# A channel gate on one pass over HBM: an early gate from one tile, loads on two queues, wide sums and a shorter last tile

## The chip, the cores and the metric

One core of a Trainium2 chip runs the kernel. The metric is device time in microseconds (us). "Span" is the time from the first to the last instruction in one profiled execution; the device time is about 1.8 us longer. All medians below are of runs on the chip, each kernel alternating with the kernel before on the same chip. A single-core program has no second die to compare with, so a run is called slow only by its time.

## The reference

```python
H = W = C = 384                      # x: (1, H, W, C) in bf16; w1d: one bf16 number
g = jnp.einsum("bhwc->bc", x) / (H * W)      # mean of each channel
s = jax.nn.sigmoid(g * w1d[0])               # k = 1: one weight
return x * s[:, None, None, :]
```

x holds 113.25 MB, and so does the output. The gate s depends on the mean of all of x, so an honest reading needs x twice: once for the mean, once for the product. Both kernels avoid the second reading. They take the mean of the first rows, compute an early gate `s_early`, multiply and store with it while the sums of the other rows go on, and at the end compare `s_early` with the true gate bit by bit in bf16. Only if they differ does a second pass run. By an estimate from the reference's inputs (x and w1d are normal numbers of spread 0.05) the gate lies so near 0.5 that one tile and all rows round to the same bf16 number.

## The kernel before

The 147,456 rows of 384 channels are cut into 1152 groups of 128 rows, one row for each partition ("rows" below are such groups; one is 768 bytes in each partition). A small planner records every operation with the memory it reads and writes and puts in the waits. The parts that matter:

```python
TILE = 45
AHEAD_TILES = 3
# ... cut ...
    sizes = split(n_rows, TILE)                   # 8 tiles of 45 rows, 18 of 44
    early_rows = sum(sizes[:AHEAD_TILES])
# ... cut ...
    def load(place, n, r0):
        plan.dma("sync", at(place, n), dram(x_rows, r0, n), writes=rows(place, n))

    def add_rows(place, n, bank, first, last):    # column sums: ones^T times each row
        for i in range(n):
            plan.op("tensor", lambda e, i=i: e.matmul(acc[bank][:, :C], ones[:], at(place + i, 1),
                    start=first and i == 0, stop=last and i == n - 1), ...)

    def put(place, n, r0):                        # gate in place, then store
        plan.op("vector", gate(place, n, s_early), ...)
        plan.final.append(
            plan.dma("scalar", dram(o_rows, r0, n), at(place, n), reads=rows(place, n)))

    ring = Ring(n_arena)                          # the room holds six tiles
    for k, n in enumerate(sizes):
        place = ring.take(n)
        while inside and any(p < place + n and place < p + m for p, m, _ in inside):
            put(*inside.pop(0))                   # gate and store the tile whose place is needed
        load(place, n, r0)
        add_rows(place, n, 0 if k < AHEAD_TILES else 1, ...)
        if k == AHEAD_TILES - 1:
            # ... copy the sums, s_early = sigmoid(sums * w / count) ...
    for tile in inside:
        put(*tile)
    # ... true sums, s_true, compare, set the flag of the second pass ...
```

Loads are issued from the sync engine's queue (q1 in the profile) and stores from the scalar engine's (q10).

## Time and profile before

| | before |
|---|---|
| device time, median of the first 3 runs | 532.59 us (532.49 to 532.88) |
| span of the profiled run | 530.9 us |
| bytes moved by DMA | 226.67 MB |
| matmuls | 1153 |
| first store issued | 55.0 us |
| last load landed | 482.8 us |

The page of the kernel before, the rows on the DMA and the engines. PE is the matmul engine, PEld its weight loads, DVE the vector engine, ACT the scalar engine and POOL the gpsimd engine, each with its busy time in us, share of the span and number of instructions; a row of a queue (q8, q14) gives packets, MB and the share of the 16 engines' time. The rows named DMA and GB/s are cut into 40 equal slices of the span: the first is the mean busy share of the 16 DMA engines in tenths, the second what they moved.

```profile
span 530.9 us, 2501 instructions
PE 241.9 (46%) x1153; PEld 127.3 (24%) x1153; DVE 236.8 (45%) x34; ACT 2.7 (1%) x4; POOL 0.3 (0%) x5
DMA  9999999999999999999999999999999999999996
GB/s 372 419 436 437 413 419 440 432 424 442 422 442 422 443 426 438 438 420 444 425 433 446 415 442 440 418 440 437 423 443 428 430 444 415 443 443 414 443 435 290
DMA packets 7502, 226.67 MB, mean 427 GB/s; under 512 B 834, under 2 KB 834, under 8 KB 834
q8 instruction: 9, 0.15, 0.1%
q14 instruction: 3, 0.02, 0.0%
```

Neither compute engine is half busy, and the DMA engines are never free. Read the DMA row before any chain of waits: the chain in this profile attributes 63% of the span to "another core or an unknown queue", which here is the time in which a store or load stood in its queue.

The windows view of the kernel before, with its line of headings; the last two numbers of a row are the DMA share and GB/s. A packet counts whole in the window in which it starts, so a share can come out a little over 1.

```profile
core 0: us, PE busy (x) PEld busy (x) DVE busy (x) ACT busy (x) POOL busy (x), PEclk, DMA share, GB/s
0.00:5.00 5.00, 0.16 (x1) 0.10 (x1) 0.39 (x3) 1.49 (x2) 0.30 (x5) 1.00 0.68 221
5.00:30.00 25.00, 15.68 (x82) 8.63 (x83) 0.00 (x0) 0.00 (x0) 0.00 (x0) 1.00 1.02 441
30.00:55.00 25.00, 18.27 (x100) 9.98 (x98) 9.77 (x3) 0.61 (x1) 0.00 (x0) 0.93 0.99 426
55.00:75.00 20.00, 9.89 (x48) 5.27 (x49) 20.00 (x3) 0.00 (x0) 0.00 (x0) 0.79 1.00 417
75.00:500.00 425.00, 197.92 (x926) 103.36 (x924) 203.73 (x23) 0.00 (x0) 0.00 (x0) 0.72 1.00 433
500.00:525.00 25.00, 0.00 (x0) 0.00 (x0) 2.87 (x5) 0.61 (x1) 0.00 (x0) 0.50 1.01 434
525.00:531.00 6.00, 0.00 (x0) 0.00 (x0) 0.00 (x0) 0.00 (x0) 0.00 (x0) 0.50 0.29 124
```

The share is 1 from 5 us to 525 us, whether loads run alone (to 55 us), loads with stores, or stores alone (after 483 us). The rate of 433 GB/s is a ceiling, not an average with holes in it. Only the first 5 us and the last 6 us are loose.

The DMA issues of the kernel before: queue, number, size, and median time from issue to landing.

```profile
arena<-in_x_dram SPq DMA_DIRECT2D x18, 4224.0 KB, 27.6
out_dram<-arena ACTq DMA_DIRECT2D x18, 4224.0 KB, 73.6
```

A load needs 27.6 us and a store 73.6, though each is 10 us of work for the 16 engines (4.325 MB / 433 GB/s). The rest is queueing; the stores are the ones that pile up.

The trace also keeps every single DMA packet with its start, duration, size and queue. A data packet here is one partition's share of a tile, 33,792 or 34,560 bytes, and takes 1251 or 1279 ns. The last packet that each of the 16 engines runs is the 4-byte semaphore write of the last store. Its end, sorted over the engines (us from the span's start; worked out from those records):

```
before  526.0 526.1 526.2 526.2 526.3 526.4 527.1 527.4 527.6 527.6 527.6 527.6 527.8 528.1 528.9 529.9
```

So the first engine is done 3.9 us before the last, and the span ends 0.9 us after the last one.

### The profile page before, as it was taken

The page shows a single profiled execution, that of the slowest core. Times are in us where ns is not written, and L with a number is a line of the kernel's source. Part 1 is how long each engine was busy: PE and PEld are TensorE (multiplying, and loading weights), DVE is VectorE, ACT ScalarE, POOL GpSimd, SP SyncE. Part 2 cuts the span into 40 slices and gives each one's busy share as a digit, 9 for nine tenths or more (in the row PEclk, how much of TensorE's full clock was granted, in tenths as well). Part 3 has the DMA queues.
Part 4 walks back from the last instruction along what each step waited for, and adds up shares of the span by engine and source line. Part 5 has one row for each costly group of instructions (what it writes and reads, how often), then busy time and mean ns, then how long its engine had stood idle before and what let it go on. Part 6 is the DMA issues. An engine that isn't in the chain of part 4 may idle for free.

```text
span 530.9 us, 2501 instructions
## 1 busy us (share of the span) xinstructions
PE 241.9 (46%) x1153; PEld 127.3 (24%) x1153; DVE 236.8 (45%) x34; ACT 2.7 (1%) x4; POOL 0.3 (0%) x5
## 2 busy tenths in 40 slices
PE   0979643326257256156156266256155265265000
PEld 0435312213123133023033133123033033133000
DVE  0005999561542642642642633642642633633800
ACT  1000000000000000000000000000000000000000
POOL 0000000000000000000000000000000000000000
PEclk9989867588576677686786775686786786676755
DMA  9999999999999999999999999999999999999996
GB/s 372 419 436 437 413 419 440 432 424 442 422 442 422 443 426 438 438 420 444 425 433 446 415 442 440 418 440 437 423 443 428 430 444 415 443 443 414 443 435 290
DMA packets 7502, 226.67 MB, mean 427 GB/s; under 512 B 834, under 2 KB 834, under 8 KB 834
## 3 DMA queue, kind: packets, MB, share of 16 engines
q1 hardware_dynamic: 3744, 113.25, 49.7%
q10 hardware_dynamic: 3746, 113.25, 49.5%
q8 instruction: 9, 0.15, 0.1%
q14 instruction: 3, 0.02, 0.0%
HBM read 113.25 MB, written 113.25 MB: 427 GB/s over the span
## 4 chain that ended last, share of the span: by engine, by line
another core or an unknown queue 63%; DMA 19%; DVE 7%; PE 3%; SPq 1%; issue 1%; ACT 0%; DVEq 0%
DMA arena<-in_x_dram 12%; DMA out_dram<-arena 8%; DVE arena L165 7%; PE acc L206 3%; SPq L91 1%; ACT s_true L273 0%; ACT s_early L255 0%; DVE total L281 0%; DVE total L249 0%; DVE wrong L289 0%; DVE total L267 0%; SPq L99 0%; DVE redo L295 0%; DVEq L99 0%
## 5 line engine op out<-in xcount | busy, mean ns | idle before, releaser
L206 PE MATMUL acc<-arena,ones 128*128 128x384 bf16 x1152 | 241.8, 381 | 248.1 <-DMA arena<-in_x_dram 248.1
L165 DVE TENSOR_TENSOR arena<-arena,s_early 128x16896 bf16<-128x16896 bf16 (+1 forms) x26 | 234.1, 9019 | 222.0 <-PE acc L206 221.3
L206 PEld LDWEIGHTS acc<-arena,ones 128*128 128x128 bf16 x1152 | 127.2, 112 | 362.3 <-DMA arena<-in_x_dram 257.8
L249 DVE COPY total<-acc 128x384 f32<-128x384 f32 x1 | 0.6, 557 | 42.1 <-PE acc L206 42.1
L273 ACT ACTIVATE s_true<-total,w_scaled 128x384 bf16<-128x384 f32 x1 | 0.6, 614 | 455.9 <-DVE total L267 455.9
L177 ACT ACT_TABLE_LOAD x1 | 1.3, 1283 | 1.3 <-PEq L373 1.3
L183 PE MATMUL acc<-w_one,ones 1*128 1x1 bf16 x1 | 0.2, 158 | 2.1 <-DMA w_one<-in_w1d_dram 2.1
L281 DVE TENSOR_TENSOR total<-s_true,s_early 128x384 f32<-128x384 uint16 x1 | 0.6, 559 | 0.7 <-ACT s_true L273 0.7
L255 ACT ACTIVATE s_early<-total,w_scaled 128x384 bf16<-128x384 f32 x1 | 0.6, 614 | 42.4 <-DVE total L249 42.4
L192 DVE TENSOR_SCALAR w_scaled<-acc 128x1 f32<-128x1 f32 x2 | 0.2, 154 | 1.3 <-PE acc L183 1.3
L183 PEld LDWEIGHTS acc<-w_one,ones 1*128 1x128 bf16 x1 | 0.1, 97 | 2.0 <-issue 2.0
L289 DVE TENSOR_REDUCE wrong<-total 128x1 f32<-128x384 f32 x1 | 0.6, 553 | 0.0
L267 DVE TENSOR_TENSOR total<-total,acc 128x384 f32<-128x384 f32 x1 | 0.5, 547 | 0.0
L173 DVE MEMSET ones<- 128x128 bf16 x1 | 0.2, 165 | 0.8 <-PEq L373 0.8
L177 ACT ACTIVATE warm<-warm 128x1 f32<-128x1 f32 x1 | 0.2, 202 | 0.0
L295 DVE CAST redo<-wrong 128x1 int32<-128x1 f32 x1 | 0.2, 154 | 0.0
L373 POOL MEMSET const-bfloat16-1.0<- 128x1 bf16 x1 | 0.1, 103 | 0.0
L373 POOL MEMSET const-uint8-127<- 128x1 uint8 x1 | 0.1, 103 | 0.0
L373 POOL MEMSET const-float32-1.0<- 128x1 f32 x1 | 0.1, 100 | 0.0
L172 POOL MEMSET warm<- 128x1 f32 x1 | 0.1, 99 | 0.3 <-POOLq L373 0.3
L373 POOL MEMSET const-float32-0.0<- 128x1 f32 x1 | 0.1, 99 | 0.2 <-issue 0.2
## 6 DMA issues: line engine op xcount, KB each, us to landing
arena<-in_x_dram SPq DMA_DIRECT2D x18, 4224.0 KB, 27.6
out_dram<-arena ACTq DMA_DIRECT2D x18, 4224.0 KB, 73.6
arena<-in_x_dram SPq DMA_DIRECT2D x8, 4320.0 KB, 30.2
out_dram<-arena ACTq DMA_DIRECT2D x8, 4320.0 KB, 58.7
w_one<-in_w1d_dram ACTq DMA_DIRECT2D x1, 0.0 KB
```

The source lines that it names most:

```text
L91: ("op", lambda e: e.dma_start(out, in_), self.pool[i], 16)
L165: return lambda e: e.tensor_tensor(v, v, s_b, ALU.mult)
L177: lambda e: e.activation(warm[:, 1:2], warm[:, 0:1], ACT_F.Sigmoid),
L183: lambda e: e.matmul(acc[2][:, 0:1], ones[0:1, :], w_one[0:1, 0:1], start=True, stop=True),
L206: lambda e, i=i: e.matmul(acc[bank][:, :C], ones[:], at(place + i, 1), start=first and i == 0, stop=last and i == n - 1,),
L249: lambda e: e.tensor_copy(total[:], acc[0][:, :C]),
L255: lambda e: e.activation(s_early[:], total[:], ACT_F.Sigmoid, scale=w_scaled[:, 0:1]),
L267: lambda e: e.tensor_tensor(total[:], total[:], acc[1][:, :C], ALU.add),
L273: lambda e: e.activation(s_true[:], total[:], ACT_F.Sigmoid, scale=w_scaled[:, 1:2]),
L281: lambda e: e.tensor_tensor(total[:], s_true[:].bitcast(U16), s_early[:].bitcast(U16), ALU.not_equal),
L289: lambda e: e.reduce_max(wrong[:], total[:], axis=mybir.AxisListType.X),
L373: nc = _bacc.Bacc("TRN2", target_bir_lowering=False, num_devices=1)
```

## The change

Its intent is to start storing sooner and to take waits out of the start and the tail. It takes `s_early` from the first tile of 44 rows; loads the first three tiles by halves on both queues; names six slots of 44 rows in place of the ring; sums 512 columns by one matmul instead of 384; makes the last two tiles 28 and 24 rows; and writes the product of the last tile into a slot that is free, so that the gate does not wait for the matmuls that read the tile.

```diff
-TILE = 45
-AHEAD_TILES = 3
+WIDE = 512
+EDGE, SLOT, BOTH = 44, 44, 3
@@ loads @@
+    def load(place, n, r0, queues=("sync",)):
+        of = dram(x_rows, r0, n)
+        i = 0
+        for queue, m in zip(queues, split(n, -(-n // len(queues)))):
+            plan.dma(queue, at(place + i, m), of[:, i * C : (i + m) * C], ...)
+            i += m
@@ sums: three banks, 512 columns each @@
-        for i in range(n):
-                    acc[bank][:, :C], ones[:], at(place + i, 1),
+        for i in range(n_wide):                      # n_wide = n * C // WIDE
+            bank = acc[group][i % 3]
+                    bank[:, :], ones[:],
+                    arena[:, start + i * WIDE : start + (i + 1) * WIDE],
@@ order @@
+    for k in range(BOTH):
+        load(places[k], sizes[k], starts[k], ("sync", "scalar"))
+    add_rows(places[0], sizes[0], 0, True, True)
+    add_banks(0, copy=True)                          # six small vector operations
+    # ... s_early ...
+    for k in range(1, len(sizes)):
+        if k >= n_slots:
+            j = k - n_slots
+            put(places[j], sizes[j], starts[j], places[j])
+        if k >= BOTH:
+            load(places[k], sizes[k], starts[k])
+        add_rows(places[k], sizes[k], 1, k == 1, k == last)
+    for k in range(len(sizes) - n_slots, last):
+        put(places[k], sizes[k], starts[k], places[k])
+    put(places[last], sizes[last], starts[last], places[last + 1 - n_slots])
```

(Shortened: some argument lists are written as "...", and the operations that compute and compare the gates are left out.)

More of the change, by code (lines that the diff above doesn't have):

```diff
@@ L108, in split @@
     return [n // k + (i < n % k) for i in range(k)]
-class Ring:
-    def __init__(self, size):
-        self.size, self.at = size, 0
-    def take(self, n):
-        if self.at + n > self.size:
-            self.at = 0
-        self.at += n
-        return self.at - n
-TILE = 45
-AHEAD_TILES = 3
+WIDE = 512
+EDGE, SLOT, BOTH = 44, 44, 3
 def bass_standalone__channel_attn_eca__vision_kernel(
@@ L134, in bass_standalone__channel_attn_eca__vision_kernel @@
     B, H, W, C = x.shape
-    assert B == 1 and C == ROW and (B * H * W) % P == 0
+    assert B == 1 and C == ROW and (B * H * W) % (4 * P) == 0
     n_rows = B * H * W // P
@@ L152, in bass_standalone__channel_attn_eca__vision_kernel @@
     arena = nc.alloc_sbuf_tensor("arena", [P, n_arena * C], BF16)
-    acc = [nc.alloc_psum_tensor(f"acc{i}", [P, 512], F32) for i in range(3)]
+    acc = [
+        [nc.alloc_psum_tensor(f"acc{g}_{i}", [P, WIDE], F32) for i in range(3)]
+        for g in range(2)
+    ]
+    w_all = nc.alloc_psum_tensor("w_all", [P, WIDE], F32)
     def at(r0, n):
@@ L160, in rows, with gate @@
         return [("sb", r) for r in range(r0, r0 + n)]
-    def gate(place, n, s):
+    def gate(to, place, n, s):
         s_b = s[:].unsqueeze(1).broadcast_to([P, n, C])
-        v = at(place, n).rearrange("p (t c) -> p t c", t=n)
-        return lambda e: e.tensor_tensor(v, v, s_b, ALU.mult)
-    sizes = split(n_rows, TILE)
-    early_rows = sum(sizes[:AHEAD_TILES])
-    plan = Planner(nc, "a", 50)
+        v, to_v = (at(r, n).rearrange("p (t c) -> p t c", t=n) for r in (place, to))
+        return lambda e: e.tensor_tensor(to_v, v, s_b, ALU.mult)
@@ new lines, in bass_standalone__channel_attn_eca__vision_kernel @@
+    n_slots = n_arena // SLOT
+    full, rest = divmod(n_rows - EDGE, SLOT)
+    if rest < EDGE:
+        full, rest = full - 1, rest + SLOT
+    sizes = [EDGE] + [SLOT] * full + [4 * q for q in split(rest // 4, EDGE // 4)]
+    assert sum(sizes) == n_rows and max(sizes) <= SLOT
+    plan = Planner(nc, "a", 50)
+    def load(place, n, r0, queues=("sync",)):
+        of = dram(x_rows, r0, n)
+        i = 0
+        for queue, m in zip(queues, split(n, -(-n // len(queues)))):
+            plan.dma(
+                queue,
+                at(place + i, m),
+                of[:, i * C : (i + m) * C],
+                writes=rows(place + i, m),
+            )
+            i += m
@@ new lines, in add_rows @@
+    def add_rows(place, n, group, first, last):
+        n_wide = n * C // WIDE
+        start = place * C
+        for i in range(n_wide):
+            bank = acc[group][i % 3]
+            plan.op(
+                "tensor",
+                lambda e, i=i, bank=bank: e.matmul(
+                    bank[:, :],
+                    ones[:],
+                    arena[:, start + i * WIDE : start + (i + 1) * WIDE],
+                    start=first and i < 3,
+                    stop=last and i >= n_wide - 3,
+                ),
+                reads=["ones"] + (rows(place, n) if i in (0, n_wide - 1) else []),
+                writes=[f"acc{group}"],
+                signal=i == n_wide - 1,
+            )
@@ new lines, in add_banks @@
+    def add_banks(group, copy):
+        for m, lo, hi in ((0, 0, C), (0, C, WIDE), (1, 0, 256), (1, 256, WIDE),
+                          (2, 0, P), (2, P, WIDE)):
+            c = (128 * m + lo) % C
+            part = total[:, c : c + hi - lo]
+            of = acc[group][m][:, lo:hi]
+            if copy and (m, lo) == (0, 0):
+                emit = lambda e, part=part, of=of: e.tensor_copy(part, of)
+            else:
+                emit = lambda e, part=part, of=of: e.tensor_tensor(
+                    part, part, of, ALU.add
+                )
+            plan.op("vector", emit, reads=[f"acc{group}", "total"], writes=["total"])
@@ new lines, in put, with weight @@
+    def put(place, n, r0, to):
+        plan.op(
+            "vector",
+            gate(to, place, n, s_early),
+            reads=["s_early"] + rows(place, n),
+            writes=rows(to, n),
+        )
+        plan.final.append(
+            plan.dma("scalar", dram(o_rows, r0, n), at(to, n), reads=rows(to, n))
+        )
+    def weight():
+        plan.op(
+            "scalar",
+            lambda e: e.activation(warm[:, 1:2], warm[:, 0:1], ACT_F.Sigmoid),
+            reads=["warm"],
+            writes=["warm1"],
+        )
+        plan.op(
+            "tensor",
+            lambda e: e.matmul(
+                w_all[:, 0:1], ones[0:1, :], w_one[0:1, 0:1], start=True, stop=True
+            ),
+            reads=["ones", "w_one"],
+            writes=["w_all"],
+        )
+        for i, n in enumerate((sizes[0], n_rows)):
+            plan.op(
+                "vector",
+                lambda e, i=i, n=n: e.tensor_scalar_mul(
+                    w_scaled[:, i : i + 1], w_all[:, 0:1], 1.0 / float(P * n)
+                ),
+                reads=["w_all"],
+                writes=[f"w_scaled{i}"],
+            )
@@ L172, in bass_standalone__channel_attn_eca__vision_kernel @@
+    starts = [sum(sizes[:k]) for k in range(len(sizes))]
+    places = [k % n_slots * SLOT for k in range(len(sizes))]
+    last = len(sizes) - 1
     plan.op("gpsimd", lambda e: e.memset(warm[:, 0:1], 0.0), writes=["warm"])
     plan.op("vector", lambda e: e.memset(ones[:], 1.0), writes=["ones"])
-    plan.dma("scalar", w_one[0:1, 0:1], w1d.unsqueeze(0), writes=["w_one"])
+    for k in range(BOTH):
+        load(places[k], sizes[k], starts[k], ("sync", "scalar"))
+        if k == 0:
+            plan.dma("scalar", w_one[0:1, 0:1], w1d.unsqueeze(0), writes=["w_one"])
@@ L175, in bass_standalone__channel_attn_eca__vision_kernel @@
+    weight()
+    add_rows(places[0], sizes[0], 0, True, True)
+    add_banks(0, copy=True)
     plan.op(
         "scalar",
-        lambda e: e.activation(warm[:, 1:2], warm[:, 0:1], ACT_F.Sigmoid),
-        reads=["warm"],
-        writes=["warm1"],
-    )
-    plan.op(
-        "tensor",
-        lambda e: e.matmul(
-            acc[2][:, 0:1], ones[0:1, :], w_one[0:1, 0:1], start=True, stop=True
-        ),
-        reads=["ones", "w_one"],
-        writes=["acc2"],
-    )
-    for i, n in enumerate((early_rows, n_rows)):
-        plan.op(
-            "vector",
-            lambda e, i=i, n=n: e.tensor_scalar_mul(
-                w_scaled[:, i : i + 1], acc[2][:, 0:1], 1.0 / float(P * n)
-            ),
-            reads=["acc2"],
-            writes=[f"w_scaled{i}"],
-        )
@@ L199, in load @@
-    def load(place, n, r0):
-        plan.dma("sync", at(place, n), dram(x_rows, r0, n), writes=rows(place, n))
-    def add_rows(place, n, bank, first, last):
-        for i in range(n):
-            plan.op(
-                "tensor",
-                lambda e, i=i: e.matmul(
-                    acc[bank][:, :C],
-                    ones[:],
-                    at(place + i, 1),
-                    start=first and i == 0,
-                    stop=last and i == n - 1,
-                ),
-                reads=["ones"] + (rows(place, n) if i in (0, n - 1) else []),
-                writes=[f"acc{bank}"],
-                signal=i == n - 1,
-            )
@@ L218, in put @@
-    def put(place, n, r0):
-        plan.op(
-            "vector",
-            gate(place, n, s_early),
-            reads=["s_early"] + rows(place, n),
-            writes=rows(place, n),
-        )
-        plan.final.append(
-            plan.dma("scalar", dram(o_rows, r0, n), at(place, n), reads=rows(place, n))
-        )
-    ring = Ring(n_arena)
-    inside = []
-    r0 = 0
-    for k, n in enumerate(sizes):
-        place = ring.take(n)
-        while inside and any(
-            p < place + n and place < p + m for p, m, _ in inside
-        ):
-            put(*inside.pop(0))
-        load(place, n, r0)
-        inside.append((place, n, r0))
-        if k < AHEAD_TILES:
-            add_rows(place, n, 0, k == 0, k == AHEAD_TILES - 1)
-        else:
-            add_rows(place, n, 1, k == AHEAD_TILES, k == len(sizes) - 1)
-        r0 += n
-        if k == AHEAD_TILES - 1:
-            plan.op(
-                "vector",
-                lambda e: e.tensor_copy(total[:], acc[0][:, :C]),
-                reads=["acc0"],
-                writes=["total"],
-            )
-            plan.op(
-                "scalar",
-                lambda e: e.activation(
-                    s_early[:], total[:], ACT_F.Sigmoid, scale=w_scaled[:, 0:1]
-                ),
-                reads=["total", "w_scaled0", "warm1"],
-                writes=["s_early"],
-            )
@@ L261, in bass_standalone__channel_attn_eca__vision_kernel @@
-    for tile in inside:
-        put(*tile)
-    plan.op(
-        "vector",
-        lambda e: e.tensor_tensor(total[:], total[:], acc[1][:, :C], ALU.add),
-        reads=["total", "acc1"],
-        writes=["total"],
-    )
+        lambda e: e.activation(
+            s_early[:], total[:], ACT_F.Sigmoid, scale=w_scaled[:, 0:1]
+        ),
+        reads=["total", "w_scaled0", "warm1"],
+        writes=["s_early"],
+    )
+    for k in range(1, len(sizes)):
[5 more added lines that the diff above has]
+        add_rows(places[k], sizes[k], 1, k == 1, k == last)
@@ L271, in bass_standalone__channel_attn_eca__vision_kernel @@
+    for k in range(len(sizes) - n_slots, last):
+        put(places[k], sizes[k], starts[k], places[k])
+    put(places[last], sizes[last], starts[last], places[last + 1 - n_slots])
+    add_banks(1, copy=False)
     plan.op(
@@ L302, in bass_standalone__channel_attn_eca__vision_kernel @@
     again = Planner(nc, "b", 50)
-    ring = Ring(n_arena)
-    r0 = 0
-    for n in sizes:
-        place = ring.take(n)
+    for place, n, r0 in zip(places, sizes, starts):
         again.dma("sync", at(place, n), dram(x_rows, r0, n), writes=rows(place, n))
@@ L309, in bass_standalone__channel_attn_eca__vision_kernel @@
             "vector",
-            gate(place, n, s_true),
+            gate(place, place, n, s_true),
             reads=rows(place, n),
@@ L316, in bass_standalone__channel_attn_eca__vision_kernel @@
         )
-        r0 += n
     for token in again.final:
```

## The prediction

> **What bounds the kernel now.** The DMA engines, from first packet to last. The page counts 226.67 MB; the windows view shows DMA share 1.00 and about 433 GB/s in nearly every 5 us stretch from 60 to 525 us, with loads and stores mixed (55 to 483) and stores alone (483 to 526). Vector is 45% busy, matmul 46%; neither is on the path. The Trainium skill, "DMA: Bandwidth & Descriptors", section "Where 436 GB/s comes from", gives 435.2 GB/s as the ceiling of the 16 ports; the trace agrees within 1%. So 226.67 MB / 433 GB/s = 523.5 us of the 530.9 us span cannot be touched: both kernels move the same bytes once.
>
> **The rest is 7.4 us.** The DMA records show it: first packet at 1.7 us; first packets take 2.0 to 2.6 us instead of 1.28; when stores start (57 us) one load packet per engine takes about 1.9 us; each of nine 16 KB fetches of PE instructions takes about 0.93 us on one engine and makes the next packet 0.4 us longer; so the engines end between 526.0 and 529.9 us, and 0.9 us more passes until the last instruction.
>
> **What the change does.**
> - Early gate from one tile: the first store's issue moves from 55 us to about 34 (tile lands near 12, 33 wide matmuls about 9.5, six small vector sums about 2.5 estimated from 0.56 for 384 columns, activation 0.6, gate 9.0). But the DMA engines were already full with six queued loads; stores only take their share sooner. The stores-only tail shrinks from 47 us to about 35 (last load lands about 493). Worth 0.
> - Two queues for three tiles: same 16 engines (same page, "Issuing engines are not separate DMA queues": it saves only issue time). An issue costs 0.33 us here, hidden behind 10 us transfers. Worth 0 to 0.3 us.
> - Six slots: the old ring also held six tiles (six loads issued without a wait). Worth 0.
> - Wide sums: 864 matmuls in place of 1152, same columns, so PE stays near 240 us, off the path. Side effect: fewer instruction fetches (9 to about 7), which trims the engine that ends last by perhaps 1 us.
> - 40 more packets per engine (halved tiles, one more tile). From 33792 B in 1251 ns and 34560 B in 1279 I estimate 19 ns fixed each: costs 0.8 us.
> - Last tile 24 rows, gated into a free slot without waiting for its sums: saves about 13 us between last load and its store's issue (matmul 8.8, gate 9.0 to 5), but some 20 MB of stores wait then, so nothing starves in either kernel. Worth 0.
> Sum: -1 us, give or take 1.5.
>
> **Prediction:** 531.3 us, range 529.3 to 533.4. Faster by over 2% 0.01, same 0.96, slower by over 2% 0.03.
>
> **What would show it.** DMA share still 1.00 and 433 GB/s from 5 to 520 us; first store issued at 30 to 38 us; last load landing at 490 to 497; loads' median time to landing rising from 28 to about 55 us and stores' falling from 73 to about 50 (slots hold waiting loads in place of waiting stores); PE busy unchanged within 10%; six or seven 16 KB instruction packets; engines' ends spread over 2 to 4 us.
>
> **What would make it wrong.** A gap in the DMA share (a queue running dry early, or near the end); packets slower than 1251 ns when mixed; the early value differing in bf16 from the true one, which would start the second pass and double the time; or a fall beyond 3 us, meaning start-up or skew losses larger than the records let me see.

## The result

The changed kernel took 531.84 us in the median of 6 runs (531.49 to 532.06 for the five fast ones, and one slow run of 540.69), against 532.61 us before (532.41 to 532.88, 6 runs). The ratio of the fast runs is 0.9985, with a 95% interval of 0.9971 to 0.9998. A ratio is the mean time of one kernel's fast runs over the mean of the other's fast runs of the same rounds, so it is not quite the ratio of the medians. "Same": 0.77 us gained, 0.15%. The outputs are right.

The same rows of the page after the change:

```profile
span 530.0 us, 1952 instructions
PE 246.4 (46%) x865; PEld 96.0 (18%) x865; DVE 241.3 (46%) x45; ACT 2.7 (1%) x4; POOL 0.3 (0%) x5
DMA  8999999999999999999999999999999999999997
GB/s 356 431 437 407 441 431 434 436 419 449 434 423 439 426 440 434 423 439 444 421 435 428 441 436 421 441 432 431 436 421 446 435 423 439 423 433 435 439 425 320
DMA packets 8220, 226.64 MB, mean 428 GB/s; under 512 B 914, under 2 KB 914, under 8 KB 914
q8 instruction: 7, 0.11, 0.1%
q14 instruction: 3, 0.02, 0.0%
```

The windows of the changed kernel, cut at its own stages: no store before 30 us, the stores set in between 30 and 45, and the last load landed at 500.

```profile
0.00:5.00 5.00, 0.00 (x0) 0.00 (x0) 0.17 (x1) 1.49 (x2) 0.30 (x5) 1.00 0.68 230
5.00:30.00 25.00, 14.61 (x60) 6.26 (x61) 5.88 (x9) 0.61 (x1) 0.00 (x0) 1.00 1.01 431
30.00:45.00 15.00, 10.93 (x38) 4.15 (x36) 14.70 (x2) 0.00 (x0) 0.00 (x0) 0.77 1.03 422
45.00:500.00 455.00, 214.14 (x752) 83.26 (x750) 211.79 (x24) 0.00 (x0) 0.00 (x0) 0.73 1.00 433
500.00:525.00 25.00, 6.70 (x18) 2.33 (x18) 8.74 (x10) 0.61 (x1) 0.00 (x0) 0.57 0.99 427
525.00:530.10 5.10, 0.00 (x0) 0.00 (x0) 0.00 (x0) 0.00 (x0) 0.00 (x0) 0.50 0.35 148
```

And its DMA issues, the whole tiles:

```profile
out_dram<-arena ACTq DMA_DIRECT2D x25, 4224.0 KB, 53.6
arena<-in_x_dram SPq DMA_DIRECT2D x22, 4224.0 KB, 47.4
```

The ceiling is the same 433 GB/s at a share of 1.00. What moved is who waits. The first store is issued at 35.9 us in place of 55.0, the last load lands at 500.1 in place of 482.8, loads wait 20 us longer in their queue, and stores 20 us less. The kernel has turned waiting stores into waiting loads; the engines that serve both were full either way.

The ends of the 16 engines:

```
before  526.0 526.1 526.2 526.2 526.3 526.4 527.1 527.4 527.6 527.6 527.6 527.6 527.8 528.1 528.9 529.9
after   526.1 526.2 526.2 526.2 526.2 526.5 526.8 527.0 527.4 527.5 527.6 527.8 527.8 528.0 528.1 529.1
```

The earliest engine ends at almost the same time (526.03 and 526.13 us); the last one ends 0.8 us sooner, which is the change of the span.

### The profile page after: what moved, and what is told of

Read it like the earlier page. It is cut to its first block, busy times and chain, and to the rows that moved or that the text cites. A ratio compares the mean times of both kernels' runs of the same rounds, so it can differ in the third digit from the quotient of the medians.

```text
span 530.0 us, 1952 instructions
## 1 busy us (share of the span) xinstructions
PE 246.4 (46%) x865; PEld 96.0 (18%) x865; DVE 241.3 (46%) x45; ACT 2.7 (1%) x4; POOL 0.3 (0%) x5
## 4 chain that ended last, share of the span: by engine, by line
another core or an unknown queue 66%; DMA 23%; PE 3%; DVE 2%; SPq 1%; issue 0%; ACTq 0%; ACT 0%; DVEq 0%
DMA arena<-in_x_dram 14%; DMA out_dram<-arena 9%; PE acc L186 3%; DVE arena L156 2%; SPq L91 1%; DVE total L208 0%; ACTq L91 0%; ACT s_true L290 0%; DVE total L298 0%; DVE wrong L306 0%; SPq L99 0%; DVE redo L312 0%; DVEq L99 0%
## 5 line engine op out<-in xcount | busy, mean ns | idle before, releaser
L186 PE MATMUL acc<-arena,ones 128*128 128x512 bf16 x864 | 246.3, 456 | 246.6 <-DMA arena<-in_x_dram 246.6
L156 DVE TENSOR_TENSOR arena<-arena,s_early 128x16896 bf16<-128x16896 bf16 (+2 forms) x27 | 234.6, 8691 | 244.8 <-PE acc L186 241.1
L186 PEld LDWEIGHTS acc<-arena,ones 128*128 128x128 bf16 x864 | 95.9, 114 | 396.5 <-DMA arena<-in_x_dram 254.8
L208 DVE TENSOR_TENSOR total<-total,acc 128x128 f32<-128x128 f32 (+2 forms) x11 | 4.5, 408 | 2.1 <-PE acc L186 1.8
## 6 DMA issues: line engine op xcount, KB each, us to landing
out_dram<-arena ACTq DMA_DIRECT2D x25, 4224.0 KB, 53.6
arena<-in_x_dram SPq DMA_DIRECT2D x22, 4224.0 KB, 47.4
```

The lines of the kernel that those rows point to most:

```text
L156: return lambda e: e.tensor_tensor(to_v, v, s_b, ALU.mult)
L186: lambda e, i=i, bank=bank: e.matmul(bank[:, :], ones[:], arena[:, start + i * WIDE : start + (i + 1) * WIDE], start=first and i < 3, stop ...
L208: emit = lambda e, part=part, of=of: e.tensor_tensor(part, part, of, ALU.add)
```

## The experiments

Two theories were tested. The first, of the prediction: the DMA engines are full throughout, none of the parts of the change touches that, and the small gain is a side effect of fewer matmul instructions, because their instructions are fetched by the same DMA engines. The rival: the parts have real gains and losses (early stores, second queue, shorter tail) that happen to cancel. Unless said otherwise each experiment edits the changed kernel, all results were correct, and "before" is the kernel before in the same rounds. The experiments ran in other rounds than the changed kernel, on three chips; there the kernel before took 532.53, 532.59 and 532.71 us, so medians of different rounds compare to about 0.2 us. The packets are those within the span, as the page counts them.

| run | edit | matmuls | 16 KB instruction packets | median us (range) |
|---|---|---|---|---|
| before | | 1153 | 9 | 532.61 |
| after | | 865 | 7 | 531.84 (531.49 to 532.06, one slow 540.69) |
| e1_sums384 | sums of 384 columns | 1153 | 9 | 532.35 (532.01 to 532.94) |
| e4_sums192 | sums of 192 columns | 2305 | 18 | 536.19 (534.53 to 540.57) |
| e5_no_sums | only the sums of two tiles | 67 | 0 | 530.2 (529.83 to 531.16, one of 536.64) |
| e5b_no_sums | the same, once more for a profile | 67 | 0 | 529.94 (one run) |
| best_pairs | rows folded on the vector engine | 289 | 2 | 530.47 (530.17 to 530.84) |
| best_pairs_one_queue | the same, first tiles on one queue | 289 | 2 | 530.5 (530.07 to 530.65) |
| e2_late | early gate from three tiles | 865 | 6 | 531.16 (531.0 to 531.35) |
| e3_one_queue | first tiles on one queue | 865 | 6 | 531.7 (531.25 to 531.75) |
| e6_last_in_place | last tile gated in place | 865 | 7 | 531.72 (531.55 to 531.78) |
| before_4slots | before, room for four tiles | 1153 | 9 | 551.01 (549.37 to 551.21) |
| after_4slots | after, four slots | 865 | 6 | 531.67 (531.21 to 533.92) |
| late_4slots | four slots, gate from three tiles | 865 | 6 | 548.34 (547.76 to 549.59) |

### Undoing the early gate, the second queue and the free slot, one at a time

```diff
 # e2_late: EARLY = 3, the early sums and their count over three tiles
-    add_rows(places[0], sizes[0], 0, True, True)
+    for k in range(EARLY):
+        add_rows(places[k], sizes[k], 0, k == 0, k == EARLY - 1)
 # e3_one_queue
-        load(places[k], sizes[k], starts[k], ("sync", "scalar"))
+        load(places[k], sizes[k], starts[k], ("sync",))
 # e6_last_in_place
-    put(places[last], sizes[last], starts[last], places[last + 1 - n_slots])
+    put(places[last], sizes[last], starts[last], places[last])
```

> The changed kernel with six slots and the early value from three tiles. Theory: first store issued at about 54 us, no gap, 531.8 us within 0.4; last load lands earlier (about 488). Rival (the early gate has a gain that another part gives back): about 1 to 3 us slower.

> The changed kernel with the first three tiles loaded whole on one queue. Theory: the same 16 engines carry it; first tile lands at about 13 to 14 us as before; 24 packets per engine fewer, which at most saves 0.2 us; 531.5 to 532.0 us. Rival (the second queue speeds the start): 0.5 us or more slower.

> The changed kernel with its last tile gated in place, so that the gate waits for the last sums. Theory: the last store is issued about 7 us later (about 512 in place of 505.6) but the store before it lands only at 523.6, so nothing is lost: 531.8 us within 0.3. Rival (the tail is on the path): about 6 us slower.

None of the three is slower than the changed kernel. Without the second queue it took 531.7 us, without the free slot 531.72. In the run with the last tile in place, the last store was issued at 511.6 us instead of 505.6, and nothing came of it: the store ahead of it in the queue lands only at about 523.6 us in the changed kernel, and the first packet of the last store starts at 520.7 us, so its issue has a slack of some 15 us. With the early gate undone the first store was issued at 57.9 us, the last load landed at 491.0, and the time was 531.16 us, 0.6 to 0.7 us less than the changed kernel; the ranges do not overlap. The expectation was 531.8 us within 0.4, so this is a small miss, though it is nearly as large as the whole gain of the change. The earliest engine ended at 526.05 us and the last one at 528.6 instead of 529.1, while the mean of the 16 ends is 527.05 against 527.15. So the difference lies in the spread of the ends, not in the steady part. The trace has six 16 KB instruction packets in place of seven, but so has the run with one queue, at 531.7 us; why the last engine ends sooner with late stores stays open. In any case no hidden gain of the early gate was found, and the rival as it was put (1 to 3 us slower) fails; a small hidden loss of the early gate, about 0.6 us, is not ruled out. The six slots and the shorter last two tiles were not undone by themselves.

### How much of the 0.8 us is instruction fetch

```diff
 # e1_sums384 and e4_sums192: NARROW = 384 or 192, one accumulator of that width per part of a row
-        n_wide = n * C // WIDE
+        n_wide = n * C // NARROW
-            bank = acc[group][i % 3]
+            bank = acc[group][i % of]             # of = C // NARROW
-                    arena[:, start + i * WIDE : start + (i + 1) * WIDE],
+                    arena[:, start + i * NARROW : start + (i + 1) * NARROW],
 # e5_no_sums: the check of the early gate is void
-        add_rows(places[k], sizes[k], 1, k == 1, k == last)
+        if k == 1:
+            add_rows(places[k], sizes[k], 1, True, True)
```

> The changed kernel with its sums back at 384 columns: 1153 matmuls in place of 865, all else as changed. Theory (the 0.8 us came from fewer instruction fetches on the DMA engines): nine 16 KB instruction packets in place of seven, span back up by 0.5 to 1 us, 532.3 to 532.9 us. Rival (it came from the early stores or the two queues): stays at 531.8 within 0.2 us.

> The changed kernel with sums of 192 columns: about 2305 matmuls. Theory: about 18 instruction packets, each costing one engine about 1.3 us, so the last engine ends 1.3 to 2.7 us later than in the changed kernel: 533 to 534.6 us. Rival (instruction fetches do not matter): 531.8 us within 0.3, as the matmul engine has time to spare.

> The changed kernel without the sums of tiles 2 to 26: the check of the early value is void, the output should still be the right one. 67 matmuls. Theory: no or one 16 KB instruction packet; engines end close together between 526.1 and about 527.5 us; 529.7 to 530.5 us. Rival: 531.8 us.

The number of 16 KB packets on the instruction queue was 18, 9, 7 and 0 in e4, e1, the changed kernel and e5, in step with the matmuls. The Trainium skill, "Runtime: NRT & Kernel Launch", section "Instruction fetch mechanics", says that an engine's instructions are refilled in blocks of 16 KiB, 256 instructions, by a DMA queue of its own. One matmul is two instructions in the profile (a weight load and a matmul), so 1152 matmuls are 2304 / 256 = 9.0 blocks and 2304 matmuls are 18.0, as counted; 864 matmuls are 6.75, and six or seven are counted. The section also calls the cost of crossing a block "mostly hidden". Whether it is hidden from the matmul engine was not tested (that engine has time to spare), but it is not hidden from a kernel that needs every DMA engine: in the kernel before each such packet held one engine for 0.88 to 0.99 us, and the data packet after it took about 1.63 to 1.69 us (once 1.83) instead of 1.25 to 1.28. That is about 1.35 us for one engine.

The page's row for this queue in the run with sums of 192 columns:

```profile
q8 instruction: 18, 0.29, 0.2%
```

The ends of the engines follow:

```
e4_sums192  526.1 526.2 526.3 526.6 526.7 526.9 527.0 528.9 529.0 529.0 529.1 529.6 530.1 531.5 531.7 532.3
e5_no_sums  526.0 526.1 526.1 526.1 526.1 526.2 526.3 526.3 526.4 526.5 526.5 526.8 526.8 526.9 527.2 527.2   (second run)
```

With 18 fetches seven engines still end before 527.1, as if they had served none, and the others end 2.8 to 6.3 us after the first, which is two to nearly five times 1.35 us. With no fetch all end within 1.2 us. Undoing the wide sums brings back 0.5 of the 0.8 us (532.35; the ranges overlap by 0.05 us). The theory holds in sign and roughly in size for 0, 7 and 9 fetches.

The records do not number the engines. But the time by which the 16 engines end after the earliest one, added up, needs no numbers: it is 6.8, 9.1, 16.3, 20.3 and 39.7 us with 0, 2 (the folding version below), 7, 9 and 18 fetches. Over the case without fetches that is 1.1, 1.3, 1.5 and 1.8 us for each, around the 1.35 us. The device time follows the last engine alone, so it also depends on which engines the fetches fall on. Where the packets can be followed from end to start along one engine, they agree: the fetch at 379.6 us of the folding version is on the engine that ends last of all, at 528.2 us.

The fetches are not all of the spread. The pages show a second instruction queue, q14, with three packets of 8 KB in both kernels and in the run without sums. In these three runs they come between 496 and 518 us, each holds an engine for 0.31 to 0.39 us, and the engine that ends last, followed back from its end, served one of them. What they fetch was not looked into.

Two misses belong here. The median with 18 fetches was above the range that had been expected: three runs gave 534.5 to 535.0, near its upper end, and three gave 537.4 to 540.6, which the fetches do not explain. And the profile of the run without sums fell on the slow execution of 536.64 us, in which many load packets all over the run took 1.4 to 2.1 us instead of 1.25 and one engine ended at 534.0. It was run again for one look:

> The kernel without sums again, for a profile: the one taken first fell in a slow execution (536.64 us beside 529.8 to 531.2), with load packets of up to 2.1 us all over the run. Theory (the engines' spread is the fetches): earliest engine ends at about 526.0, latest by 528, 529.7 to 530.2 us. Rival (without the sums the DMA packets themselves go slower): slow load packets again, later earliest end.

It took 529.94 us with the ends shown above and no such packets after 45 us, so the slow packets are not the work of that kernel. The kernel before had one run of 538.48 us too in these rounds, and it was counted among its fast runs; the ratios of these rounds are therefore a little low, and the medians are compared instead. What slows such executions stays open.

### When would an early gate pay?

If six tiles can be loaded before any room is needed, the loads fill the engines until about 63 us (six times 10.2 us after a start at 1.7), and a first store at 55 us is early enough. With room for four tiles the loads should end at 45 us, as the fourth load does in the kernel before.

```diff
 # before_4slots
-    n_arena = nc.sbuf_bytes_remaining // (2 * C)
+    n_arena = 4 * TILE
 # after_4slots and late_4slots
-    n_slots = n_arena // SLOT
+    n_slots = 4
 # late_4slots also has the edit of e2_late
```

> The kernel before with room for four tiles (ring of 180 rows). Theory (early gate is worth nothing only because six tiles can be loaded before the first store): four loads are done at about 45 us, the first store is issued at about 55, so the DMA share falls to 0 for 10 to 13 us; about 545 us (542 to 549). Rival (the start of the stores never matters): 532.6 us within 1.

> The changed kernel with four slots. Theory: first store issued at about 36 us, while the fourth load still runs until about 45, so no gap: 531.8 us within 1. Rival (fewer slots hurt by themselves): as much slower as the kernel before with four slots.

> The changed kernel with four slots and the early value again taken from three tiles. Theory: a gap in the DMA share of 10 to 13 us, about 545 us (542 to 549), as in the kernel before with four slots. Rival (one of the other parts of the change, last tile or two queues, covers for it): 532 us.

Windows of the kernel before with room for four tiles, around the first store and around the end:

```profile
35.00:45.00 10.00, 9.60 (x44) 5.14 (x45) 0.00 (x0) 0.00 (x0) 0.00 (x0) 0.73 0.79 339
45.00:55.00 10.00, 7.86 (x48) 4.32 (x45) 8.91 (x2) 0.61 (x1) 0.00 (x0) 1.00 0.00 0
55.00:65.00 10.00, 0.00 (x0) 0.00 (x0) 10.00 (x3) 0.00 (x0) 0.00 (x0) 0.63 0.90 387
520.00:530.00 10.00, 6.86 (x37) 3.68 (x35) 3.04 (x1) 0.00 (x0) 0.00 (x0) 0.91 1.00 427
530.00:540.00 10.00, 0.00 (x0) 0.00 (x0) 7.65 (x5) 0.61 (x1) 0.00 (x0) 0.60 0.47 203
```

The same windows of the changed kernel with four slots:

```profile
35.00:45.00 10.00, 8.75 (x32) 3.59 (x33) 10.00 (x2) 0.00 (x0) 0.00 (x0) 0.83 1.04 417
45.00:55.00 10.00, 6.07 (x17) 2.29 (x18) 9.33 (x2) 0.00 (x0) 0.00 (x0) 0.66 1.00 433
55.00:65.00 10.00, 3.67 (x17) 1.47 (x15) 6.22 (x1) 0.00 (x0) 0.00 (x0) 0.79 1.00 433
```

And of the changed kernel with four slots and the gate from three tiles:

```profile
35.00:45.00 10.00, 9.10 (x34) 3.81 (x36) 0.14 (x1) 0.00 (x0) 0.00 (x0) 0.83 0.76 323
45.00:55.00 10.00, 6.94 (x33) 2.94 (x30) 9.15 (x7) 0.61 (x1) 0.00 (x0) 0.96 0.00 0
55.00:65.00 10.00, 0.00 (x0) 0.00 (x0) 10.00 (x2) 0.00 (x0) 0.00 (x0) 0.50 0.76 324
```

Between 45 and 55 us the DMA share is 0.00 in both kernels that wait for three tiles: four tiles are loaded, none is gated yet, and no room is free. The kernel before loses 2.1 + 10 + 1.0 = 13.1 us there. The changed kernel with four slots has no such hole and takes 531.67 us, the same as with six. So the early gate does what it was meant to do; in this kernel, with six tiles of room, there was no hole to close.

The kernel before lost more than had been expected, 551.0 us against 542 to 549. A second hole explains it, at 530 to 540 us (share 0.47, 5.3 us lost). The chain that ended last, its pieces around the last tile (start, duration, what):

```profile
489.92 27.44 DMA arena<-in_x_dram
517.40 9.47 PE acc L206 x44
526.96 8.96 DVE arena L165
```

With four tiles of room the stores that wait are not enough to cover 18.4 us of sums and gate after the last load. 13.1 + 5.3 = 18.4 us, against 18.2 us of longer span. So close a match is partly luck: the windows show another loss, 411 GB/s from 65 to 100 us, and a gain beside it, since the ends of the engines lie 1.2 us apart here in place of 3.9. Here the free slot and the small last tiles of the change would count as well: late_4slots, which has them, has only the first hole to a large extent and took 2.7 us less. Its window at the same place:

```profile
530.00:540.00 10.00, 3.78 (x13) 1.34 (x11) 6.25 (x10) 0.61 (x1) 0.00 (x0) 0.84 0.95 406
```

Those parts were not tried one by one with four slots.

### A version that is faster than both

If fetches cost time, matmuls should go. The vector engine has time: it folds each 44-row tile to 22 and then to 11 rows by two bf16 additions into a scratch area, the gate of the tile follows at once, and the matmul engine sums 11 rows. One slot is given up for the scratch.

```diff
-    n_slots = n_arena // SLOT
+    n_slots = n_arena // SLOT - 1
@@ add_rows, now called just before the put of the same tile @@
+        work = n_slots * SLOT + turn[0] % 2 * half
+        for src, m in ((place, n // 2), (work, n // 4)):
+            plan.op("vector", lambda e, src=src, m=m: e.tensor_tensor(
+                at(work, m), at(src, m), at(src + m, m), ALU.add), ...)
-        for i in range(n_wide):
+        for i in range(n // 4):                    # one matmul for each folded row
```

> A try at a better version: the vector engine folds each 44-row tile to 11 rows (two bf16 additions), so 289 matmuls are left; five slots and a scratch area; the gate no longer waits for the matmuls. Theory: two or three instruction packets; vector busy about 400 us, still under 20 us a tile, so DMA share stays 1.00; 530.0 to 531.2 us. If the vector engine falls behind (a tile over 20 us) the time rises by several us or more.

> The folding version with the first three tiles loaded whole on one queue. Theory: 24 packets fewer per engine at about 7 ns each, 0.2 us off 530.5: 530.1 to 530.5 us. Rival (the second queue helps this version, whose first sums start sooner): 0.3 us or more slower than the folding version.

The page of the folding version:

```profile
span 529.0 us, 841 instructions
PE 95.0 (18%) x289; PEld 38.9 (7%) x289; DVE 415.6 (79%) x89; ACT 2.7 (1%) x4; POOL 0.3 (0%) x5
DMA  8999999999999999999999999999999999999998
q8 instruction: 2, 0.03, 0.0%
```

It took 530.47 us in the median of 6 runs, about 2.1 us less than the kernel before and 1.4 us less than the changed kernel, with no overlap of the ranges; at 0.4 and 0.3% it is still "same". It also gates without waiting for the matmuls and has one slot less, so that the whole gain is fetches is not shown. With one queue for the first tiles it took 530.5 us (ratio to before 0.9959, 0.9946 to 0.9971), so the second queue is worth nothing here either. The vector engine is 79% busy and still not on the path. The true mean is now made of sums of two and of four rows rounded to bf16, a coarser check of the early gate than before. The kernel without sums, at 530.2 us, shows that little is left below that.

## Why the prediction was right

The predicted time was 531.3 us (529.3 to 533.4) and the measured one 531.84; a gain of 1 us give or take 1.5 was foreseen and 0.77 came. The number alone proves little. The range would have held no change at all (532.6 us), and the sum was loose: the terms as written (1 us gained by fetches, 0 to 0.3 by the second queue, 0.8 lost to more packets) add to a gain of 0.2 to 0.5 us, not 1, and the 531.3 us stand for 1.3. That it came so near is partly luck; what speaks for the prediction is the mechanism, part by part.

- **The bound.** Right: share 1.00 and 433 GB/s in both kernels for loads, stores and the mixture. The Trainium skill's 435.2 GB/s ("DMA: Bandwidth & Descriptors", "Where 436 GB/s comes from") is half a percent above the trace.
- **Early gate worth nothing.** Right in that it gains nothing: undoing it costs nothing with six slots. Undoing it even saved 0.6 to 0.7 us (531.16 us), which was not foreseen and is not explained. The four-slot runs show the mechanism: 548.3 us with a late gate, 531.7 with an early one.
- **Two queues worth nothing.** Right: 531.7 us without. The same page, "Issuing engines are not separate DMA queues", says so, and the traces agree: 434 GB/s from 5 to 30 us with the loads on one queue, 431 on two.
- **Tail worth nothing.** Right for the free slot: 6 us later issue of the last store, no change (531.72 us). The shorter last tiles were not undone.
- **Fewer fetches worth perhaps 1 us.** Right in kind, somewhat large: seven packets in place of nine, the last engine ends 0.8 us sooner, and undoing the wide sums costs 0.5 us.
- **More packets cost 0.8 us.** Mis-sized. I took 19 ns of fixed time a packet from two nearly equal sizes. The half tiles gave a better lever: 16,896 bytes in 629 ns and 33,792 in 1251, so (1251 - 629) is the price of 16,896 bytes and 7 ns are left over. For 40 packets that is an estimated 0.28 us, and the earliest engine ended 0.1 us later.
- **Last load at 490 to 497 us, loads at 55 us to landing, stores at 50.** Wrong in size: 500.1, 47.4 and 53.6. Two things were missed. A store issued into the load stream does not start at once: issued at 35.9, its first packets started at 40.7 us, and 48 load packets, three for each engine, started in between. (With the engines idle, in before_4slots, the wait was 0.9 us: issued at 55.8, started at 56.7.) That moves every later load issue. And the two queues take turns by packet, not by byte: the last tiles have load packets of 21,504 and 18,432 bytes (799 and 686 ns) against store packets of 1251 ns, so eight of each take 16.4 and 15.5 us. The last loads landed 16.4 and 15.5 us apart (468.2, 484.6, 500.1), where equal bytes would have given 12.7 and 10.9. Neither moves the end, because the engines stay full.

## What to carry to other kernels

When the DMA share is 1.00 from end to end, divide the bytes by the measured rate before valuing any change: here 523.5 of 530.9 us could not be touched, and reordering loads and stores only changed which of them waits. In these runs an early start of the stores paid only where the loads would otherwise run out of room first, so compare the time to fill the room (slots times load time) with the time to the first store. For the last microseconds look at when each DMA engine ends, and at everything that uses them besides your data, the instruction stream included.

## What the Trainium skill lacked or had wrong

- "Runtime: NRT & Kernel Launch", "Instruction fetch mechanics": it calls instruction fetch mostly hidden. In a DMA-bound kernel each 16 KB block took one DMA engine 0.88 to 0.99 us, plus about 0.4 us on the next data packet; 0, 7, 9 and 18 blocks went with 530.2, 531.8, 532.4 and 534.5 us or more. The page does not say that the cost lands on the data engines.
- "DMA: Bandwidth & Descriptors", "Where 436 GB/s comes from": the note there that the HBM side, about 358 GB/s, binds for transfers between HBM and SBUF does not hold for one core alone; loads, stores and mixtures ran at 433 GB/s. (The page's own table of measurements and "HBM Reference" have about 425 GB/s for a lone core.)
- "DMA: Bandwidth & Descriptors", "Queues, rings and completion order": turns between queues by packet are confirmed, but not what follows from it, that a queue with smaller packets gets fewer bytes: with 18,432 against 33,792 bytes a load took 15.5 us where equal bytes would give 10.9.
- No page has the wait of the first packet of a store on a queue that stood empty, beside a queue full of loads: 4.8 us after issue in the changed kernel (35.9 to 40.7) and 4.4 us in the one before (55.0 to 59.4), against 0.9 us with the engines idle (before_4slots).
